# Retention and two feed-forward layers on one core: the second layer's first product by seven block products in place of eight

## The chip, the cores and the metric

The kernel runs on 1 of the 8 cores of one Trainium2 chip. The metric is the device time of one execution in microseconds (us), lower is better; the value before is the median of three runs. Of one execution a hardware profiler also left a trace, and all rows below come from it.

## The reference

Retention over two batches, then two dense layers with an activation between the products. The second layer is what the change touches.

```python
# retention: state = gamma*state + k v^T ; y = q state / 8      (2 batches, 8 heads, 768 positions, 64)
x = attn_out.transpose(0, 2, 1, 3).reshape(1536, 512)
h = x @ w_in          # layer 1: 512 -> 2048
x = (np.maximum(h, 0.0) + np.log1p(np.exp(-np.abs(h)))) @ w_out        # 2048 -> 512
h = x @ w_in2         # layer 2, first product: 512 -> 2048
g = h * np.clip(h + 3.0, 0.0, 6.0) / 6.0
out = g @ w_out2      # layer 2, second product: 2048 -> 512
```

The weights arrive as 64-bit floats.

## The kernel before, in words

One large function, `tile_retention_moe_kernel`, does not issue instructions. It gives tasks to a planner (class `Plan`, lines 25 to 124): each has an engine, a cost, the tasks it follows, a due time, and the buffer slots that it takes and gives back. `Plan.run` then places the tasks by these costs and due times, which fixes the order of the instructions on each engine. Every engine takes its list in that order, and waits where an operand is not there yet. All instructions are recorded by one helper, so line 44 stands in every row and the names of the tiles tell operations apart.

**Precision.** Each operand of a product is held as two 32-bit parts, hi and lo, and a product of 128 x 128 weights with 512 columns is three matmuls: hi·hi, hi·lo, lo·hi. Making the parts costs two instructions for each 128 x 512 tile: ScalarE copies (`hi`), VectorE subtracts (`lo`).

**The layers.** Tokens are cut into three chunks of 512 (`NC`), the inner width 2048 into 16 slices `f` of 128. A unit is a layer, a chunk and a slice: `G1` (line 658) is the first product, 4 x 3 = 12 matmuls of 512 columns into one PSUM bank; then ScalarE and VectorE form the activation `g` and its hi and lo; `G2` (line 693) is the second product, again 12 matmuls, added up in four banks over the 16 slices. TensorE's order is a list (lines 231 to 250): G1 of unit s, G2 of unit s - 2, through all 96 units, with the retention in the gaps of layer 1. The last two G2 are merged by row block `j`; behind each row block VectorE scales the sums from PSUM into one of two `e` tiles (`scaled`, line 736) and a DMA stores it (line 739). An `e` tile is free again when its store has landed.

**Weights.** `weight` (line 265) fetches 512 KB of 64-bit words into one of three `raw` slots, takes some six instructions on ScalarE and VectorE to make a 32-bit word of them in one of four `cv` slots, and splits that into hi and lo in a `w` slot. In layer 2 the lo part is made by ScalarE (the negative) and an accumulating DMA of GpSimd's queue. All 64 weight slices stay in SBUF from then on; a slot of layer 1 becomes free when its last unit is done.

## Time and profile before

| what | value |
|---|---|
| device time, median of 3 runs | 586.13 us (586.0 to 586.29) |
| span of the profiled execution, first to last instruction | 584.8 us |
| TensorE busy | 576.6 us, 3607 matmuls |
| VectorE busy | 325.6 us |
| ScalarE busy | 302.5 us |
| GpSimd busy | 60.6 us |
| moved by DMA | 57.49 MB |

The profile gives the profiled execution's span alone; the median of the runs lies 1.33 us above it, which is what stands around the first and last instruction. Busy time is summed over the durations of instructions, and instructions of one engine overlap at their ends: a matmul of 512 columns lasts 0.39 us in a row, but the next one starts earlier than that. So a pace is read from starts, not from durations. The idle time before a row, in brackets, names what ended it.

### The profile page before, as it was taken

How to read it: one execution, taken by the hardware profiler on the slowest of the kernel's cores; microseconds unless marked ns; L12 is line 12 of the kernel's file. 1: busy time of each engine (PE TensorE's matmuls, PEld its weight loads, DVE VectorE, ACT ScalarE, POOL GpSimd, SP SyncE). 2: the span in 40 equal slices, each digit the busy share in tenths (PEclk: the TensorE clock that was granted, in tenths of full speed). 3: DMA queues.
4: the chain of work that ended last, by engine and by line, in shares of the span. 5: the costliest groups of instructions: out<-in, count | busy, mean ns of one | idle time of the engine just before them, and what ended most of it. 6: DMA issues, size and time to landing. Idle time of an engine off the chain costs nothing.

```text
span 584.8 us, 9136 instructions
## 1 busy us (share of the span) xinstructions
PE 576.6 (99%) x3607; PEld 474.5 (81%) x3607; DVE 325.6 (56%) x579; ACT 302.5 (52%) x503; POOL 60.6 (10%) x93
## 2 busy tenths in 40 slices
PE   8999999999999999999999999999999999999997
PEld 7778788887788788888888888888888888888886
DVE  4999999886655333666678776422422222422222
ACT  3589989883233333777799997622222222222220
POOL 0000001044440000011121221100000000000000
PEclk9999999999999999999999999999999999999999
DMA  9998766513442200265597798200100000100001
GB/s 198 253 262 210 195 182 210 170 31 68 82 81 68 73 1 0 55 156 141 137 244 173 199 245 218 49 6 0 73 1 1 1 1 0 73 0 1 0 1 72
DMA packets 75242, 57.49 MB, mean 98 GB/s; under 512 B 47552, under 2 KB 64960, under 8 KB 75200
## 3 DMA queue, kind: packets, MB, share of 16 engines
q1 hardware_dynamic: 68336, 46.42, 28.2%
q0 software_dynamic: 6864, 10.49, 10.4%
q8 instruction: 28, 0.46, 0.4%
q14 instruction: 14, 0.11, 0.1%
HBM read 44.05 MB, written 3.15 MB: 81 GB/s over the span
## 4 chain that ended last, share of the span: by engine, by line
PE 97%; DVE 2%; DMA 0%; issue 0%; ACT 0%; POOL 0%; DVEq 0%; ACTq 0%; POOLq 0%
PE banks L44 97%; DVE raw L44 0%; DVE cv L44 0%; DMA out_dram<-e 0%; ACT w L44 0%; DVE e L44 0%; DVE st L44 0%; DVE qT L44 0%; DVE pw L44 0%; DVE w L44 0%; DVE x_lo L44 0%; DVEq L788 0%; POOL ident masks.py:199 0%; POOL small masks.py:65 0%; DVEq L44 0%
## 5 line engine op out<-in xcount | busy, mean ns | idle before, releaser
L44 PE MATMUL banks<-x_hi,w 128*128 128x512 f32 x768 | 252.9, 392 | 0.0
L44 PEld LDWEIGHTS banks<-x_hi,w 128*128 128x128 f32 x768 | 144.0, 188 | 30.6
L44 PE MATMUL banks<-x_lo,w 128*128 128x512 f32 x384 | 149.0, 389 | 0.0
L44 PE MATMUL banks<-hi,w 128*128 128x512 f32 x384 | 126.9, 392 | 0.0
L44 PE MATMUL banks<-w,hi 128*128 128x512 f32 (+1 forms) x386 | 118.4, 388 | 0.0
L44 DVE SCALAR_TENSOR_TENSOR g<-e,banks 128x512 f32<-128x512 f32 x48 | 33.0, 688 | 123.4 <-ACT e L44 123.2
L44 ACT ACTIVATE e<-banks,three 128x512 f32<-128x512 f32 x48 | 32.8, 684 | 120.2 <-PE banks L44 112.7
L44 DVE TENSOR_TENSOR lo<-g,hi 128x512 fp32r<-128x512 f32 x96 | 66.1, 689 | 41.4 <-ACT hi L44 41.2
L44 PEld LDWEIGHTS banks<-hi,w 128*128 128x128 f32 x384 | 72.1, 188 | 15.4
L44 PEld LDWEIGHTS banks<-w,hi 128*128 128x128 f32 x386 | 72.4, 188 | 14.9
L44 PEld LDWEIGHTS banks<-x_lo,w 128*128 128x128 f32 x384 | 72.2, 188 | 14.5
L44 ACT ACTIVATE hi<-g 128x512 fp32r<-128x512 f32 x96 | 60.4, 629 | 44.9 <-DVE g L44 42.2
L44 PE MATMUL banks<-w,lo 128*128 128x512 f32 (+1 forms) x193 | 74.9, 388 | 0.0
L44 PE MATMUL banks<-lo,w 128*128 128x512 f32 x192 | 74.8, 390 | 0.0
L44 DVE SCALAR_TENSOR_TENSOR cv<-raw,cv 128x512 uint32<-128x512 uint32 x96 | 65.8, 688 | 1.6
L44 ACT ACTIVATE w<-cv 128x512 fp32r<-128x512 f32 x101 | 60.2, 624 | 12.3 <-DVE cv L44 11.9
L44 POOL DMA_DIRECT2D w<-cv x37 | 32.6, 880 | 285.9 <-ACT w L44 166.5
L44 ACT ACTIVATE g<-banks 128x512 f32<-128x512 f32 x48 | 28.4, 591 | 59.1 <-PE banks L44 59.1
L44 ACT ACTIVATE cv<-raw,half 128x512 uint32<-128x512 uint32 x64 | 48.5, 759 | 3.5 <-DMA raw<-in_moe_w_out_dram 2.2
L44 DVE TENSOR_SCALAR raw<-raw 128x512 f32<-128x512 f32 x96 | 40.7, 428 | 10.8 <-ACT raw L44 7.9
L44 PEld LDWEIGHTS banks<-w,lo 128*128 128x128 f32 x193 | 36.2, 188 | 7.5
L44 PEld LDWEIGHTS banks<-lo,w 128*128 128x128 f32 x192 | 36.0, 188 | 7.2
(60 smaller groups left out, 367.1 us busy)
## 6 DMA issues: line engine op xcount, KB each, us to landing
raw<-in_moe_w_in_dram SPq DMA_DIRECT2D x32, 512.0 KB, 4.2
raw<-in_moe_w_out_dram SPq DMA_DIRECT2D x32, 512.0 KB, 4.6
w<-cv POOLq DMA_DIRECT2D x37, 256.0 KB, 4.9
out_dram<-e SPq DMA_DIRECT2D x11, 256.0 KB, 2.0
q<-in_q_dram SPq DMA_DIRECT2D x8, 256.0 KB, 5.3
v<-in_v_dram SPq DMA_DIRECT2D x8, 256.0 KB, 5.2
k<-in_k_dram SPq DMA_DIRECT2D x7, 256.0 KB, 5.4
raw<-in_k_dram SPq DMA_DIRECT2D x4, 256.0 KB, 3.4
```

The lines of the kernel that those rows point to most:

```text
L44: return self.plan.tc.keep_in_program_order(getattr(self.engine, op)(*args, **kwargs))
```

## The change

Layer 1 and the retention stay. In layer 2 the units of 512 tokens go, and there are 16 **steps** in their place: two blocks of 768 tokens, times eight pairs of slices `f`; block 0 takes the pairs 0 to 7, block 1 takes them from 7 to 0. In a step the first product is a 2 x 2 by 2 x 2 block product (two slices of 128, two halves of the 512 inputs, two halves of 384 tokens) by Strassen's scheme: seven products P1 to P7 of 6 matmuls with 384 columns, on sums of blocks. This asks for:

- sums of the weights (`late_in`: four VectorE instructions of 256 columns, then four hi/lo pairs), sums of the inputs (`operands`: four VectorE instructions of 768 columns and seven hi/lo pairs for each block of tokens; the rows of layer 1's result are copied once by ScalarE, without a split);
- in each step three additions that put the seven products together in two PSUM banks and in SBUF, and the activation in pieces: ten VectorE and six ScalarE instructions in all (a1 to a5, d1 to d9 and the hi/lo pairs `parts`);
- the second product as 12 `unit`s of 3 matmuls with 512 columns, which TensorE does between the products of the next step; it adds up in six PSUM banks, so each block ends with six output tiles, through the same two `e` tiles.

The second layer's weights no longer all stay in SBUF: the 16 slices of the second product are made in the `raw` slot itself (`late_out`), stored to a DRAM scratch, and read back for each block; the sums of pairs 0 to 3 (`KEEP`) are stored and read back for block 1. The lo parts of layer 2's weights are now made by VectorE; the 32 accumulating DMAs for them are gone.

```diff
--- before.py
+++ after.py
-        if kind == "h":
+        if kind in ("h", "prod"):
             return [[0], [1]]
+        if kind == "out":
+            return [[2 + u]]
...
+    G = [(0, c, f) for c in range(NC) for f in range(NF)]
+    STEPS = [(b, p) for b in range(2) for p in (range(NPAIR) if b == 0 else reversed(range(NPAIR)))]
+    PRODUCTS = {"P1": 2, "P6": 2, "P2": 2, "P7": 2, "P5": 2, "P4": 1, "P3": 1}
...
+    behind = [("G2", len(G) - LAG + i) for i in range(LAG)]
+    for i in range(len(STEPS)):
+        for name, n in PRODUCTS.items():
+            pe += [(name, i)] + behind[:n]
+            behind = behind[n:]
+        behind = [("unit", i, n) for n in range(12)]
+    pe += behind
...
+    def late_out(f):
+
+
+        key = 1, 1, f
+        x = Words(1, key, words[1][1])
+        at = due["P1", f // 2] - 40.0 + 2.0 * f
+        t = x.made(at, at - 10.0, 1.45, [])
+
+        def part(i):
+            return x.flat()[:, i * CH:(i + 1) * CH].bitcast(F32R)
+
+        a = nc.add("ACT", ACS, lambda: nc.scalar.activation(part(0), x.w().bitcast(F32), AF.Copy), [t], at)
+        b = nc.add("DVE", TT, lambda: nc.vector.tensor_tensor(part(1), x.w().bitcast(F32), part(0).bitcast(F32), ALU.subtract), [a], at + 0.7, give=[x.cv_k])
+        home = kept(f"stash_out{f}")
+        c = nc.add("SP", 0.45, lambda: nc.sync.dma_start(out=home, in_=x.flat().bitcast(F32)), [a, b], at + 1.5, give=[x.raw_k], load=1.6)
+        for b in range(2):
+            i = STEPS.index((b, f // 2))
+            back(("wo", b, f), home, c, due["unit", i, 3 * (f % 2)] - 12.0)
+
+    def back(key, home, after, when):
+        T["W", key] = [nc.add("SP", 0.45, lambda: nc.sync.dma_start(out=at_slot(key).rearrange("p a n -> p (a n)").bitcast(F32), in_=home),
+                              [after], when, take=[("w", key)], load=1.6, hold=HOLD + when - 10.0)]
+
+    def late_in(p):
+
+
+        x = [Words(1, (1, 0, 2 * p + f), words[1][0]) for f in range(2)]
+        at = due["P1", p] - (20.0 if p else 12.0)
+        t = [v.made(at + 2 * f, at - 10.0 + f, 1.75, [v.raw_k]) for f, v in enumerate(x)]
...
+        s1 = nc.add("DVE", d, put(0, lambda: word(1, 0), lambda: word(1, 1), ALU.add), t, at + 3.0, take=[sums])
+        s3 = nc.add("DVE", d, put(2, lambda: word(0, 0), lambda: word(1, 0), ALU.subtract), [s1], at + 3.1)
+        s2 = nc.add("DVE", d, put(1, lambda: total(0), lambda: word(0, 0), ALU.subtract), [s1], at + 3.2)
+        s4 = nc.add("DVE", d, put(3, lambda: word(0, 1), lambda: total(1), ALU.subtract), [s2], at + 3.3)
...
+        for n, (source, cols, after, give) in enumerate((
+                (lambda: x[0].w().bitcast(F32), whole, t, [x[0].cv_k]),
+                (lambda: x[1].w().bitcast(F32)[:, halves[1]], halves[1], t, [x[1].cv_k]),
+                (lambda: pair(0), whole, [s1, s2], [sums[1]]),
+                (lambda: pair(2), whole, [s3, s4], [sums[1]]))):
...
+            if p < KEEP:
+                home = kept(f"stash_in{p}_{n}")
+                c = nc.add("SP", 0.45, lambda home=home, key=key: nc.sync.dma_start(out=home, in_=at_slot(key).rearrange("p a n -> p (a n)").bitcast(F32)),
+                           [a, b], at + 6 + n, give=[key], load=1.6)
+                i = STEPS.index((1, p))
+                back(("wi", 1, p, n), home, c, due["P1", i] - 15.0 + n / 10)
...
+    def operands(b):
...
+        put(1, lambda: x(0, 1), lambda: x(0, 0), ALU.subtract, before, when["P6"] - 2.5)
+        put(2, lambda: x(1, 1), lambda: tf(1), ALU.subtract, [made[1]], when["P6"] - 1.5)
+        put(3, lambda: x(1, 1), lambda: x(0, 1), ALU.subtract, before, when["P7"] - 1.5)
+        put(4, lambda: x(1, 0), lambda: tf(2), ALU.subtract, [made[2]], when["P4"] - 1.5)
...
+            a = nc.add("ACT", act(2 * QT), lambda key=key, source=source: nc.scalar.activation(at_slot(key)[:, 0], source(), AF.Copy),
+                       [made[n]] if give else before, when[name], take=[("xf", key)], give=give, hold=early)
+            d = nc.add("DVE", dve(2 * QT), lambda key=key, source=source: nc.vector.tensor_tensor(
+                at_slot(key)[:, 1], source(), at_slot(key)[:, 0].bitcast(F32), ALU.subtract), [a], when[name] + 0.9, give=give)
...
+    A_OF = {"P1": (0, 0), "P2": (0, 1), "P3": (3, 1), "P4": (1, 1), "P5": (2, 0), "P6": (2, 1), "P7": (3, 0)}
+    BANK = {"P1": 1, "P2": 1, "P6": 2, "P7": 3, "P4": 3, "P5": 4, "P3": 4}
+
+    def step(i):
...
+                for kk in range(2):
+                    for m, (l, r) in enumerate(((0, 0), (0, 1), (1, 0))):
+                        first = fresh and kk == 0 and m == 0
+                        nc.tensor.matmul(bank(BANK[name]), w[:, l, kk, :], x[:, r, kk, :], start=first, stop=kk == 1 and m == 2, skip_group_check=not fresh)
+
...
+        p1 = product("P1", [])
+        p6 = product("P6", [])
+        a1 = ac(QT, lambda: nc.scalar.activation(at_slot(first), bank(1), AF.Copy), [p1], D["P2"] - 2.0, [first], psum=True)
+        p2 = product("P2", [a1])
+        d1 = dv(QT, lambda: nc.vector.tensor_tensor(at_slot(mid), at_slot(first), bank(2), add), [p6, a1], D["P7"] - 1.2, [mid], [first, K(2)])
+        p7 = product("P7", [])
+        a2 = ac(QT, lambda: nc.scalar.activation(at_slot(e[0])[:, 0], bank(1), AF.Relu, bias=three), [p2], D["P5"] - 1.8, [e[0]], psum=True)
+        d4 = dv(QT, lambda: nc.vector.scalar_tensor_tensor(at_slot(c[0])[:, 0], at_slot(e[0])[:, 0], 6.0, bank(1), ALU.min, ALU.mult), [a2], D["P5"] - 1.0, [c[0]], [K(1)])
+        p5 = product("P5", [])
+        d2 = dv(QT, lambda: nc.vector.tensor_tensor(at_slot(total), at_slot(mid), bank(3), add), [p7, d1], D["P4"] - 1.2, [total])
+        p4 = product("P4", [d2])
+        d3 = dv(QT, lambda: nc.vector.tensor_tensor(at_slot(c[0])[:, 1], at_slot(total), bank(4), add), [p5, d2, d4], D["P3"] - 1.2, [], [total])
+        p3 = product("P3", [d3])
+        a3 = ac(QT, lambda: nc.scalar.activation(at_slot(e[0])[:, 1], at_slot(c[0])[:, 1], AF.Relu, bias=three), [d3], after_all - 2.5)
+        d5 = dv(QT, lambda: nc.vector.scalar_tensor_tensor(at_slot(c[0])[:, 1], at_slot(e[0])[:, 1], 6.0, at_slot(c[0])[:, 1], ALU.min, ALU.mult), [a3], after_all - 1.8, [], [e[0]])
+        d7 = dv(QT, lambda: nc.vector.tensor_tensor(at_slot(c[1])[:, 1], at_slot(mid), bank(3), add), [p4, d2], after_all - 0.5, [c[1]], [mid, K(3)])
+        d8 = dv(QT, lambda: nc.vector.tensor_tensor(at_slot(c[1])[:, 0], at_slot(mid), bank(4), add), [p3, d3, d7], after_all, [], [mid, K(4)])
+        a5 = ac(2 * QT, lambda: nc.scalar.activation(at_slot(e[1]), at_slot(c[1]), AF.Relu, bias=three), [d7, d8], after_all + 0.6, [e[1]])
+        d9 = dv(2 * QT, lambda: nc.vector.scalar_tensor_tensor(at_slot(c[1]), at_slot(e[1]), 6.0, at_slot(c[1]), ALU.min, ALU.mult), [a5], after_all + 1.2, [], [e[1]])
+        for n, after, when in ((0, [d4, d5], after_all - 1.0), (1, [d9], after_all + 2.0)):
+            a = ac(2 * QT, lambda n=n: nc.scalar.activation(at_slot(g[n])[:, 0], at_slot(c[n]), AF.Copy), after, when, [g[n]], [c[n]])
+            d = dv(2 * QT, lambda n=n: nc.vector.tensor_tensor(at_slot(g[n])[:, 1], at_slot(c[n]), at_slot(g[n])[:, 0].bitcast(F32), ALU.subtract), [a], when + 0.9, [], [c[n]])
+            T["parts", i, n] = [a, d]
+
...
+        for n in range(12):
+            q, x = divmod(n, 6)
+            f, t = (0, x) if x < 3 else (1, x)
+            if q:
+                f, t = (0, x + 3) if x < 3 else (1, x - 3)
...
+            u = nc.add("PE", UNIT, go, T["parts", i, q] + T["W", w_key], at, take=[("bank", key)] if begun else [], give=[g[q], w_key])
...
```

**The order on TensorE**, in layer 2. Before, G1 of a unit (`x_hi`, `x_lo`) is followed by G2 of an earlier one (`w` with `hi` and `lo`):

```order
L44 MATMUL banks<-x_hi_1721,w_100 128x512 x2
L44 MATMUL banks<-x_lo_1724,w_100 128x512
L44 MATMUL banks<-x_hi_1721,w_100 128x512
L44 MATMUL banks<-w_1369,hi_107 128x512 x2
L44 MATMUL banks<-w_1369,lo_110 128x512
```

Of the change, the begin of step 2: P1 and P6, P2, P7, P5 (`xf` with `w`) with two units of step 1 (`w` with `parts`) behind each:

```order
L44 MATMUL banks<-xf_2871,w_96 128x384 x6
L44 MATMUL banks<-w_1354,parts_3261 128x512 x6
L44 MATMUL banks<-xf_2911,w_101 128x384 x6
L44 MATMUL banks<-w_1354,parts_3261 128x512 x3
L44 MATMUL banks<-w_1376,parts_3261 128x512 x3
L44 MATMUL banks<-xf_2886,w_96 128x384 x6
L44 MATMUL banks<-w_1376,parts_3261 128x512 x6
L44 MATMUL banks<-xf_2952,w_1330 128x384 x6
L44 MATMUL banks<-w_1354,parts_3157 128x512 x6
L44 MATMUL banks<-xf_2890,w_101 128x384 x6
L44 MATMUL banks<-w_1354,parts_3157 128x512 x3
L44 MATMUL banks<-w_1376,parts_3157 128x512 x3
```

The second products that stood as 12 matmuls in a row now stand in threes and sixes between products. Step 0 has no step before it: there, P6, P2, P7, P5, P4, P3 of step 0 and P1, P6 of step 1 follow each other with nothing between.

**The order on VectorE**, in layer 2. Before, with the weights done, two instructions for a unit (`g`, the activation, and `lo`):

```order
L44 SCALAR_TENSOR_TENSOR g_105<-e_102,banks 128x512
L44 TENSOR_TENSOR lo_110<-g_105,hi_107 128x512
L44 SCALAR_TENSOR_TENSOR g_104<-e_103,banks 128x512
L44 TENSOR_TENSOR lo_109<-g_104,hi_106 128x512
```

Of the change, step 4, from its addition d3 (`c` from `total`) to d8 (the second `c` from `part`); `raw` and `cv` are weights being made, `sums` their sums, `parts_3261` the lo part of the activation's first half:

```order
L44 TENSOR_TENSOR c_3112<-total_3121,banks 128x384 [waits PE_49]
L44 SCALAR_TENSOR_TENSOR cv_2_76<-raw_1_70,cv_2_76 128x512 [waits DVE_49]
L44 TENSOR_TENSOR sums_2458<-cv_1_75 128x256
L44 TENSOR_TENSOR sums_2458<-cv_3_77,cv_1_75 128x256
L44 SCALAR_TENSOR_TENSOR c_3112<-e_0_3109,c_3112 128x384 [waits Activation_49]
L44 TENSOR_TENSOR sums_2458<-sums_2458,cv_3_77 128x256 [waits DVE_49]
L44 TENSOR_TENSOR sums_2458<-cv_3_77,sums_2458 128x256 [waits DVE_49]
L44 TENSOR_SCALAR raw_2_71<-raw_2_71 128x512 [waits DMAHW3_49,Activation_49]
L44 SCALAR_TENSOR_TENSOR cv_0_74<-raw_2_71,cv_0_74 128x512 [waits DVE_49]
L44 TENSOR_TENSOR c_3144<-part_3099,banks 128x384 [waits PE_49]
L44 TENSOR_TENSOR parts_3261<-c_3112,parts_3261 128x768 [waits Activation_49]
L44 TENSOR_TENSOR c_3144<-part_3099,banks 128x384 [waits PE_49]
```

The making of weights, which stood beside units of two instructions, now stands inside steps of ten, and an instruction for a weight that waits for its fetch (`DMAHW3`) has the step's additions queued behind it.

**The end, on VectorE.** Before, the last four output tiles; the waits on a DMA are for the `e` tile:

```order
L44 TENSOR_SCALAR e_103<-banks 128x512 [waits PE_49]
L44 TENSOR_SCALAR e_102<-banks 128x512 [waits PE_49]
L44 TENSOR_SCALAR e_103<-banks 128x512 [waits DMAHW2_49,DVE_49,PE_49]
L44 TENSOR_SCALAR e_102<-banks 128x256 [waits DMAHW3_49,DVE_49,PE_49]
L44 TENSOR_SCALAR e_102<-banks 128x256
```

Of the change, the last six:

```order
L44 TENSOR_SCALAR e_103<-banks 128x512 [waits DMAHW2_49,PE_49]
L44 TENSOR_SCALAR e_102<-banks 128x512 [waits DMAHW3_49,PE_49]
L44 TENSOR_SCALAR e_103<-banks 128x512 [waits DMAHW0_49,DVE_49,PE_49]
L44 TENSOR_SCALAR e_102<-banks 128x512 [waits DMAHW1_49,DVE_49,PE_49]
L44 TENSOR_SCALAR e_103<-banks 128x512 [waits DMAHW2_49,DVE_49,PE_49]
L44 TENSOR_SCALAR e_102<-banks 128x256 [waits DMAHW3_49,DVE_49,PE_49]
L44 TENSOR_SCALAR e_102<-banks 128x256
```

Six tiles pass through the two `e` tiles where four did, and the six become ready at the ends of six units in a row.

## Rows read from the trace of the kernel before

**Rows 1.** The page: busy time of the engines, and the chain by engine.
```profile
PE 576.6 (99%) x3607; PEld 474.5 (81%) x3607; DVE 325.6 (56%) x579; ACT 302.5 (52%) x503; POOL 60.6 (10%) x93
...
PE 97%; DVE 2%; DMA 0%; issue 0%; ACT 0%; POOL 0%; DVEq 0%; ACTq 0%; POOLq 0%
```

**Rows 2.** Waits of TensorE: total us, times, longest us.
```profile
PE banks L44 <- ACT w L44: 2.1, 2, 1.1
PE banks L44 <- POOL ident masks.py:199: 1.5, 1, 1.5
PE banks L44 <- DVE qT L44: 1.0, 1, 1.0
```

**Rows 3.** Timeline, TensorE's last matmuls: start us, us, engine, operation, count.
```profile
575.87 0.39 PE L44 MATMUL banks<-w,lo 128*128 128x512 f32 x1
...
576.55 0.39 PE L44 MATMUL banks<-w,lo 128*128 128x512 f32 x1
...
580.17 0.40 PE L44 MATMUL banks<-w,hi 128*128 128x256 f32 x2
...
580.41 0.28 PE L44 MATMUL banks<-w,lo 128*128 128x256 f32 x1
580.41 0.31 PEld L44 LDWEIGHTS banks<-w,hi 128*128 128x128 f32 x2
580.53 0.40 PE L44 MATMUL banks<-w,hi 128*128 128x256 f32 x2
...
580.77 0.28 PE L44 MATMUL banks<-w,lo 128*128 128x256 f32 x1
```

**Rows 4.** Groups by line: weight loads; count, busy us and mean ns, idle before.
```profile
L44 PEld LDWEIGHTS banks<-w,hi 128*128 128x128 f32 x386 | 72.4, 188 | 14.9
```

**Rows 5.** Timeline, VectorE at the end: the output tiles.
```profile
576.97 0.69 DVE L44 TENSOR_SCALAR e<-banks 128x512 f32<-128x512 f32 x1 [1.22 <-PE banks L44]
...
579.83 0.69 DVE L44 TENSOR_SCALAR e<-banks 128x512 f32<-128x512 f32 x1 [0.80 <-DMA out_dram<-e]
...
581.22 0.76 DVE L44 TENSOR_SCALAR e<-banks 128x256 f32<-128x256 f32 x2 [0.70 <-DMA out_dram<-e]
```

**Rows 6.** A group of VectorE with 256 columns; then the timeline of one unit's activation.
```profile
L44 DVE TENSOR_TENSOR st<-st,banks 128x256 f32<-128x256 f32 x16 | 6.7, 417 | 0.8 <-PE banks L44 0.2
...
572.95 0.69 ACT L44 ACTIVATE e<-banks,three 128x512 f32<-128x512 f32 x1 [3.36 <-PE banks L44]
...
573.67 0.69 DVE L44 SCALAR_TENSOR_TENSOR g<-e,banks 128x512 f32<-128x512 f32 x1 [3.36 <-ACT e L44]
...
574.40 0.63 ACT L44 ACTIVATE hi<-g 128x512 fp32r<-128x512 f32 x1 [0.76 <-DVE g L44]
```

**Rows 7.** Timeline of VectorE, a stretch with no idle time between instructions.
```profile
300.11 0.69 DVE L44 SCALAR_TENSOR_TENSOR cv<-raw,cv 128x512 uint32<-128x512 uint32 x1
300.72 0.43 DVE L44 TENSOR_SCALAR raw<-raw 128x512 f32<-128x512 f32 x1
301.18 0.69 DVE L44 SCALAR_TENSOR_TENSOR cv<-raw,cv 128x512 uint32<-128x512 uint32 x1
301.79 0.42 DVE L44 TENSOR_SCALAR e<-g 128x512 uint32<-128x512 uint32 x1
302.13 0.69 DVE L44 SCALAR_TENSOR_TENSOR cv<-raw,cv 128x512 uint32<-128x512 uint32 x1
```

**Rows 8.** Stretches: length; busy us of PE, PEld, DVE, ACT, POOL; clock, DMA, GB/s.
```profile
30.00:60.00 30.00, 29.01 (x324) 22.97 (x324) 29.79 (x61) 28.64 (x49) 0.11 (x1) 1.00 0.86 234
60.00:100.00 40.00, 40.00 (x422) 32.24 (x417) 37.70 (x76) 35.38 (x61) 3.03 (x4) 1.00 0.69 188
```

**Rows 9.** DMA from 300 to 350 us: queue; fetches, KB, us to landing.
```profile
q1 hardware_dynamic: 3908, 7.31, 45.5%
...
raw<-in_moe_w_out_dram SPq DMA_DIRECT2D x10, 512.0 KB, 4.8
...
raw<-in_moe_w_in_dram SPq DMA_DIRECT2D x4, 512.0 KB, 5.4
```

More of the change, by code (lines that the diff above doesn't have):

```diff
@@ L128 @@
 GEMM = 2.73
+PRODUCT, UNIT = 1.03, 0.69
 SIGN = 0.75
@@ L334, in weight @@
+        part = [("w0" if number < ONCE else "w", ("w", key))]
         tail = 1.5 if BY_DVE(number) else 7.0
[L335 to L345 removed]
@@ L719, in gemm2 @@
[L719 to L722 removed]
+                for n, (l, r) in enumerate(((wh, hi), (wh, lo), (wl, hi))):
+                    nc.tensor.matmul(at_slot(("acc", c, j)), l[:, sl], r, start=(f == 0 and n == 0), stop=(f == NF - 1 and n == 2))
```

331 lines of the change are left out of this document (209 added, 122 removed).

## The prediction

> **What bounds the kernel now.** I read the page's busy times and chain first, then TensorE's waits, then single rows for prices. TensorE is busy for 576.6 us and has 97% of the chain [rows 1]; its three waits sum to 4.6 us [rows 2]. So the time is TensorE's list of matmuls and a tail: its last matmul ends at 580.77 + 0.28 = 581.05 [rows 3], 3.75 us before the span ends at 584.8. A shorter list is a gain only as far as no new wait enters it. The median of the runs, 586.13, lies 1.33 above the span; I add the terms to the span and carry the 1.33 along.
>
> **The list gets shorter: -14.1 us.** The pace comes from starts: three matmuls of 512 columns take 576.55 - 575.87 = 0.68 us, 0.2267 each, and five of 256 columns 580.77 - 580.17 = 0.60 us, 0.120 each [rows 3]. The line through both is 0.417 ns a column, the full one of the two clock levels, 2.4 GHz (granted share 1.00 in [rows 8]), plus 13 ns. For 384 columns no row exists; the line gives 0.1733 us. The bounds are 0.160 (columns alone) and 0.188, the mean of one weight load [rows 4], if loads should not hide. I take the line: in [rows 3] two loads start and end within 0.31 us while matmuls follow at 0.120, so loads of 188 ns overlap. The first product of layer 2 is 48 x 12 = 576 matmuls, 576 x 0.2267 = 130.6 us; with the change 16 x 7 x 6 = 672, 672 x 0.1733 = 116.5 us. The second product has 576 matmuls of 512 columns in both: nothing. A step is 42 x 0.1733 + 36 x 0.2267 = 15.44 us.
>
> **The tail gets longer: +2.8 us.** Output tiles pass through two `e` tiles, and a tile's next use comes 579.83 - 576.97 = 2.86 us after its last [rows 5], held by its store. Before, tiles are ready every 1.36 us, so two in 2.86 is nearly the pace. Now six end at units 0.68 us apart. With the first scaling at 0, the second starts at 0.68, the third at 2.86, the fourth at 3.54, the fifth at 5.72, the sixth at 6.40; from that start the span ends 584.8 - 581.22 = 3.58 later [rows 5], at 9.98. TensorE ends 5 x 0.68 = 3.4 after the first, so the tail is 6.58 in place of 3.75.
>
> **Step 0 has no cover: +1.1 us.** The parts of a chain: a hand-over is some 0.04 us (572.95 + 0.69 to 573.67) [rows 6]. VectorE takes 0.69 for 512 columns and 0.42 for 256 [rows 6], so 0.56 for 384 and 0.96 for 768. No row has ScalarE at another size: 384 lie between 0.52 (in proportion to 0.69) and 0.69; I take VectorE's share, 0.57, and so 0.87 for 768 (from 0.63). P5 needs the bank of P2: the end of P2 comes 0.17 after the next product can start (0.39 - 0.2267), then a2 and d4 with hand-overs, 0.17 + 0.09 + 0.57 + 0.04 + 0.56 + 0.1 = 1.53. Between stands P7 alone, 1.04: a wait of 0.5. P6 of step 1 waits 0.1 for a bank in the same way, and unit 0 stands 0.5 too early, since d3, a3, d5 and the pair `parts` (0.56, 0.57, 0.56, 0.87, 0.96) run with weights between them. In later steps two units (1.36) stand in each gap and these waits vanish: unit 0 comes 5.8 after the end of P5, and that chain takes 4.1.
>
> **VectorE in block 0: +2.5 us, between 0 and 10.8.** It fills up. At full load the next instruction starts 0.60 after one of 512 columns (300.11 to 300.72), 0.34 after a `TENSOR_SCALAR` (301.79 to 302.13), and 0.46 after it if its result is needed (300.72 to 301.18) [rows 7]. For 256 it is 0.76 - 0.42 = 0.34 [rows 5, 6], so 0.47 for 384 and 0.87 for 768. From d1 of step 1 to d1 of step 6 the list has 28, 24, 29, 32 and 31 instructions: 15.3, 12.2, 15.4, 16.7 and 16.1 us, and 23 of them need the result just before (0.12 each), in all 78.5 us. TensorE's five steps take 77.2. Steps 4 and 5 alone need 34.1 for 30.9. d1 may be late by some 3.2 without harm (P6 is followed by two units, P2 and two units, 3.8, before P7 needs d1), so load alone costs nearly nothing; but the list is in order, and each step also waits a little for TensorE or ScalarE, about 1 us, 5 in all. 78.5 + 5 - 77.2 - 3.2 = 3.1; I take 2.5, because in [rows 8] a VectorE at 29.79 of 30 us cost TensorE 1.0 and one at 37.70 of 40 nothing, which for 77 us is 1 to 2.5. The upper end takes full durations in place of starts (0.69, 0.43, 0.56, 0.42, 0.96; 88.0 us): 88.0 - 77.2 = 10.8.
>
> **What I cost at nothing.** Steps 9 to 15: ten VectorE instructions, 7 x 0.47 + 3 x 0.87 = 5.9 of 15.44 us. The last step: its second half of `parts` is ready some 4.6 after P3 (d8, a5, d9 and the pair, with hand-overs), under one unit of step 14 and six of its own (4.76); without this cover TensorE would wait those 4.6 once. The last nine units of layer 1, where the weights now begin: 78 instructions of VectorE, 43.4 us by the same paces, in 9 x 5.44 = 49. ScalarE: 82 instructions from step 1 to 6, about 60 us even at full durations, in 77. The 32 accumulating DMAs that go were off the path (GpSimd busy 10%) [rows 1]. The DMAs: 32 fetches, 32 stores and 16 reads of 512 KB, 41.9 MB, before block 0 ends, in about 149 us (nine units and 6.5 steps). The SP queue moved 7.31 MB in 45.5% of 50 us [rows 9], 0.321 MB/us, so these need 131: hidden, but not by much. They are hidden by a lead: the sums of pair p are done in step p - 2, some 23 us before use. If the lead is used up, each late transfer counts its 4.8 or 5.4 us.
>
> **Sum.** 584.8 - 14.1 + 2.8 + 1.1 + 2.5 = 577.1 of span, **578.4 us** as the runs are timed, 1.3% less.
>
> **Rivals.** *All covered* (0.20): VectorE's lateness stays within the 3.2, and step 0 costs little; 584.8 - 14.1 + 2.8 + 1.33 = 574.8. For it: [rows 8], 60 to 100. Against it: 78.5 us in 77.2. *VectorE sets block 0's pace* (0.10): the waits of a list in order add up as if nothing overlapped; 578.4 + 10.8 - 2.5 = 586.7 at most, 582 at least. Against it: the starts in [rows 7]. *The three `raw` slots set the pace, slower* (0.08): a slice of the second product now keeps its slot through a fetch (4.8), six conversions and a split (some 4.5) and its store (3.5, an estimate by doubling the bytes of an output's 2), 12.8; a slice of the first 5.4 + 3.2 = 8.6. Two of each a pair are 42.8, over three slots 14.3 of 15.44. From 1.2 us more for each slot's use this decides; with 4 more on engines that are full it is 19.6 a pair, 4.2 a step, 33 in eight, less the lead of 23: 578.4 + 10 = 588.4. For it: the SP queue is in order, and a fetch that waits for a store holds back the reads behind it. *Weight loads don't hide, slower* (0.04): 672 x 0.188 = 126.3, a gain of 4.2 for 14.1; 578.4 + 9.9 = 588.3. It decides from 0.174 us a load; [rows 3] speak against it with 0.120. The Trainium skill has a rule for this side, on its page "TensorE: Matmul & The Clock Gate", section "Back-to-back issue gap": a stream of loads and matmuls is paced by both, at about 131 ns for 512 columns and 81 for 128. By it, an estimate, 384 columns take 114, 672 x 0.114 = 76.8 against 576 x 0.131 = 75.5, so the product would become longer by 1.3 and the time 593.8. The trace doesn't agree: 512 columns take 227 here.
>
> **How the numbers follow.** My forecast has 0.58, from 575.5 to 581.5. The range leaves out the two slower rivals and the upper half of *VectorE sets the pace*, 0.17: 574.0 (all covered, with the end a little shorter) to 585.0. A change of 0.2%, 1.2 us, is about what a measurement of this kernel can tell from none. Faster by more: 0.58 + 0.20 + 0.06 (the lower part of the third case) = 0.84; the same 0.04; slower 0.08 + 0.04 = 0.12.
>
> **What would show it.** Right: starts of 384-column matmuls 0.173 apart; steps 9 to 15 at 15.4 us; a tail of 6.6 us behind the last matmul with two or three `e` scalings that wait for `out_dram`; a wait of about half a microsecond at P5 of step 0; in steps 4 and 5 a few waits of TensorE for `part` or `parts` by VectorE, 1 to 5 us in all. Wrong: 0.188 apart (weight loads); TensorE waiting for `w` by a DMA, or VectorE idle before `raw` rows for a fetch (slots); block 0 steps of 17 us (VectorE).

## The result, and the profile after

The changed kernel takes **580.53 us** (median of 4 runs, 579.83 to 581.24) against 586.21 us of the kernel before, timed beside it (586.0 to 586.54): a ratio of 0.9904, 95% interval 0.989 to 0.9918. The profiled execution took 580.47 us, with a span of 578.7. The forecast was 578.4 us, and a span of 577.1.

The page of the kernel after: the engines' busy time, and the chain by engine, to be read beside [rows 1].

```profile
PE 566.5 (98%) x3703; PEld 482.9 (83%) x3703; DVE 409.3 (71%) x733; ACT 311.0 (54%) x505; POOL 32.8 (6%) x61
...
PE 81%; DVE 9%; DMA 6%; ACT 2%; issue 1%; SPq 0%; DVEq 0%; ACTq 0%
```

TensorE has 96 matmuls more and is busy for 10.1 us less; VectorE has 84 us more to do. The chain no longer is TensorE's alone: 9% and 6% of it run through VectorE and DMAs.

TensorE's waits after (total us, times, longest us), beside [rows 2]:

```profile
PE banks L44 <- ACT w L44: 2.0, 2, 1.1
PE banks L44 <- POOL ident masks.py:199: 1.5, 1, 1.5
PE banks L44 <- DVE qT L44: 1.0, 1, 1.0
PE banks L44 <- DVE c L44: 0.6, 2, 0.4
```

The three old waits stand as they were, in layer 1. One line is new: VectorE's `c`. The timeline of TensorE (start us, us, engine, operation, count, and in brackets the idle time and its releaser) shows where:

```profile
313.83 0.87 PE L44 MATMUL banks<-xf,w 128*128 128x384 f32 x4
...
323.91 2.37 PE L44 MATMUL banks<-xf,w 128*128 128x384 f32 x12 [0.19 <-DVE c L44]
...
389.19 0.86 PE L44 MATMUL banks<-w,parts 128*128 128x512 f32 x3
390.41 1.31 PE L44 MATMUL banks<-xf,w 128*128 128x384 f32 x6 [0.36 <-DVE c L44]
...
405.52 0.86 PE L44 MATMUL banks<-w,parts 128*128 128x512 f32 x3
406.51 1.32 PE L44 MATMUL banks<-xf,w 128*128 128x384 f32 x6
```

Layer 2 begins at 313.83 with P1 of step 0 (before it began at 314.29, so 0.46 of the gain lies ahead of the change and is no more than the 0.9 by which this moment differs between the profiles of this study). The other rows are P5 of step 0, and P1 of steps 5 and 6 with the unit before each. A bracket counts from the end of the matmul before, which overlaps the next one; by starts P5 comes 0.36 late, and the two P1 come 1.22 and 0.99 after a unit that elsewhere takes 0.70, so 0.52 and 0.29 late. From start to start of P1 the steps take 13.32 us (step 0, with the last two second products of layer 1 in place of units), 15.67 to 15.69 (1 to 3), 16.21 (4), 16.10 (5), 15.76 (6), and 15.69 in every step from 7 to 14. In steps 4 to 6 the planner has put some units later than the list (in step 4 P6 stands straight behind P1). In a step of 15.69 nothing is idle, by the view of stretches (length; busy us of PE, PEld, DVE, ACT, POOL; clock, DMA share, GB/s), the last row being step 12:

```profile
327.16:406.51 79.35, 78.86 (x391) 70.26 (x390) 73.00 (x136) 50.11 (x83) 0.00 (x0) 1.00 0.65 223
...
500.71:516.40 15.69, 15.69 (x80) 14.10 (x79) 6.58 (x11) 4.32 (x6) 0.00 (x0) 1.00 0.58 202
```

TensorE is busy for all of the 15.69 us at full clock, while VectorE and ScalarE do 6.58 and 4.32 us. Yet 42 x 0.1733 + 36 x 0.2267 is 15.44. So 0.25 us of each step is neither a wait nor in the list as priced. In fifteen steps that is 3.7 us, more than all of TensorE's listed waits in layer 2. It is the main question of the experiments; the second is what delayed steps 4 to 6, the third the tail. VectorE's output tiles, beside [rows 5]:

```profile
568.44 1.37 DVE L44 TENSOR_SCALAR e<-banks 128x512 f32<-128x512 f32 x2 [0.97 <-PE banks L44]
571.32 1.36 DVE L44 TENSOR_SCALAR e<-banks 128x512 f32<-128x512 f32 x2 [1.51 <-DMA out_dram<-e]
574.24 1.40 DVE L44 TENSOR_SCALAR e<-banks 128x512 f32<-128x512 f32 x3 [1.56 <-DMA out_dram<-e]
```

Two tiles, a wait for a store, two tiles, a wait, the last two (one of them in halves): the pairs start 2.88 and 2.92 us apart. TensorE's last matmul ends at 571.83, and the span 6.87 us after it.

### The profile page after: what moved, and what is told of

Read it like the earlier page. It is cut to its first block, busy times and chain, and to the rows that moved or that the text cites. A ratio compares the mean times of both kernels' runs of the same rounds, so it can differ in the third digit from the quotient of the medians.

```text
span 578.7 us, 9565 instructions
## 1 busy us (share of the span) xinstructions
PE 566.5 (98%) x3703; PEld 482.9 (83%) x3703; DVE 409.3 (71%) x733; ACT 311.0 (54%) x505; POOL 32.8 (6%) x61
## 4 chain that ended last, share of the span: by engine, by line
PE 81%; DVE 9%; DMA 6%; ACT 2%; issue 1%; SPq 0%; DVEq 0%; ACTq 0%
PE banks L44 81%; DMA raw<-in_moe_w_in_dram 3%; DVE cv L44 3%; DVE c L44 2%; DVE raw L44 1%; DMA stash_out<-raw 1%; DVE parts L44 1%; DVE w L44 1%; DMA out_dram<-e 1%; DVE sums L44 1%; DMA q<-in_q_dram 1%; DMA raw<-in_moe_w_out_dram 1%; ACT raw L44 1%; ACT e L44 0%; DVE e L44 0%
## 5 line engine op out<-in xcount | busy, mean ns | idle before, releaser
L44 PE MATMUL banks<-w,parts 128*128 128x512 f32 x579 | 149.6, 392 | 0.0
L44 PE MATMUL banks<-xf,w 128*128 128x384 f32 x672 | 134.5, 337 | 0.7 <-DVE c L44 0.6
L44 PEld LDWEIGHTS banks<-xf,w 128*128 128x128 f32 x672 | 120.1, 188 | 10.9 <-DVE c L44 1.9
L44 PE MATMUL banks<-x_hi,w 128*128 128x512 f32 x384 | 127.3, 395 | 0.0
L44 PEld LDWEIGHTS banks<-w,parts 128*128 128x128 f32 x579 | 106.9, 188 | 16.0
L44 PEld LDWEIGHTS banks<-x_hi,w 128*128 128x128 f32 x384 | 72.0, 188 | 15.6
L44 PE MATMUL banks<-x_lo,w 128*128 128x512 f32 x192 | 74.4, 390 | 0.0
L44 DVE SCALAR_TENSOR_TENSOR g<-g,e 128x512 f32<-128x512 f32 x48 | 33.0, 687 | 13.1 <-ACT e L44 12.8
L44 PEld LDWEIGHTS banks<-x_lo,w 128*128 128x128 f32 x192 | 36.1, 188 | 7.0
L44 DVE TENSOR_TENSOR lo<-g,hi 128x512 fp32r<-128x512 f32 x48 | 33.0, 687 | 8.3 <-ACT hi L44 8.2
```

The lines of the kernel that those rows point to most:

```text
L44: return self.plan.tc.keep_in_program_order(getattr(self.engine, op)(*args, **kwargs))
```

## The experiments

Ratios are to the kernel before, timed beside each.

### One product more: is it TensorE's list that counts?

```diff
-                for kk in range(2):
+                for kk in (0, 1, 0, 1) if name == "P3" else (0, 1):
```

> Edit: the six matmuls of product P3 are issued twice in each of the 16 steps, so that its sum counts it double; all else is the same. It puts back on TensorE one product of the eight that the scheme replaces. If TensorE's list sets the time in every step (theory A): 16 x 6 x 0.1733 = 16.6 us more, less what the waits in block 0 (about 0.8 us) give back, so 596.3 to 597.1 us. If VectorE or the fetches set the pace of block 0 (rival B: there the longer step gives them room), the eight steps of block 0 grow by less than 1.04 us each, and the time lies under 593.

One execution took 596.64 us, 16.2 more than the changed kernel's profiled execution, and the last matmul ends 16.2 later too (588.05). Of these 16.2, 0.64 lies ahead of layer 2, which begins at 314.47 here. The product adds 1.01 to 1.04 us to each of steps 1 to 3 and 7 to 14: there TensorE's list sets the time. In steps 4 to 6 it does not come out in full: they take 16.73, 16.77 and 16.69 us, so 0.52, 0.67 and 0.93 more. The waits before P1 of steps 5 and 6 are gone, 1.0 us in all, as theory A's "less what the waits in block 0 give back" has it. So block 0's other work was about 1 us behind TensorE's list there, and what is missing of the forecast in the other steps must lie in how fast the list runs.

### The quarter of a microsecond in each step

**One column count.** The units of the second product leave out 128 of their 512 columns, so that all matmuls of layer 2 have 384.

```diff
-                for cs in halves if tail else [slice(0, CH)]:
+                for cs in [slice(0, QT)]:
...
-                        nc.tensor.matmul(..., start=begun and m == 0, stop=ended and m == 2 and cs.stop == CH)
+                        nc.tensor.matmul(..., start=begun and m == 0, stop=ended and m == 2)
```

> Leaves out the last 128 of the 512 columns of each matmul of the second layer's second product, so that all 78 matmuls of a step have 384 columns; the tail's halves go too. In the changed kernel steps 10 to 14 take 15.69 us each where 42 x 0.1733 + 36 x 0.2267 = 15.44 was forecast. Theory, a change of column count costs (some 0.034 us for each pair of changes, seven pairs a step): with one size the steps take 78 x 0.1733 = 13.52 us and all starts are 0.173 apart. Rival, it is the operands (slices of wide tiles, other banks) or the reads and writes of the other engines beside them: the extra 0.25 us stays, 13.77 us a step.

561.02 us in one execution. Steps 10 to 14 take 13.52 us each, which is 78 x 0.1733 to the last digit. Its timeline, in step 13:

```profile
505.79 1.20 PE L44 MATMUL banks<-xf,w 128*128 128x384 f32 x6
506.83 1.20 PE L44 MATMUL banks<-w,parts 128*128 128x384 f32 x6
507.87 1.20 PE L44 MATMUL banks<-xf,w 128*128 128x384 f32 x6
```

Six matmuls in 1.04 us, 0.1733 each, products and units alike. So the line through 256 and 512 columns was right for 384, weight loads hide, and the second product's data do not cost. The same stretch of the changed kernel, step 12:

```profile
504.20 1.55 PE L44 MATMUL banks<-w,parts 128*128 128x512 f32 x6
505.59 1.21 PE L44 MATMUL banks<-xf,w 128*128 128x384 f32 x6
506.64 1.55 PE L44 MATMUL banks<-w,parts 128*128 128x512 f32 x6
...
513.94 0.86 PE L44 MATMUL banks<-w,parts 128*128 128x512 f32 x3
514.64 1.22 PE L44 MATMUL banks<-xf,w 128*128 128x384 f32 x6
515.70 0.86 PE L44 MATMUL banks<-w,parts 128*128 128x512 f32 x3
```

Six of 512 columns take 505.59 - 504.20 = 1.39 instead of 1.36, three take 0.70 instead of 0.68, six of 384 take 1.05 to 1.06 instead of 1.04. Wherever the column count changes, the next run is a little longer than its pace. But for the halves of the last unit the order of the instructions on every engine is the same in both kernels, so it is not the change of operands or of banks.

**Fewer changes.** The order after has seven pairs of changes in a step (a run of products, a run of units, seven times). Gathered into four:

```diff
-    PRODUCTS = {"P1": 2, "P6": 2, "P2": 2, "P7": 2, "P5": 2, "P4": 1, "P3": 1}
+    PRODUCTS = {"P1": 0, "P6": 4, "P2": 0, "P7": 4, "P5": 0, "P4": 3, "P3": 1}
```

> The whole computation, TensorE's order alone: P1 P6, four units, P2 P7, four units, P5 P4, three units, P3, one unit, so four pairs of changes between 384 and 512 columns in a step where there were seven. Theory, a change of column count costs: the extra 0.25 us a step falls to about 0.14, steps 10 to 14 take 15.58 us, and the time falls by some 1.6 us to 578.9, unless P6, which now follows P1 at once, waits for its bank. Rival, operands or traffic: steps stay at 15.69 us, time 580.5.

581.72 us (580.96 to 582.36), ratio 0.992 (0.9905 to 0.9935). Steps 7 to 14 take 15.68: a miss, nearly all of the extra stays. In step 4, at P6, and in step 12:

```profile
376.87 1.34 PE L44 MATMUL banks<-xf,w 128*128 128x384 f32 x6 [0.53 <-DVE c L44]
...
502.65 2.26 PE L44 MATMUL banks<-xf,w 128*128 128x384 f32 x12
504.75 2.92 PE L44 MATMUL banks<-w,parts 128*128 128x512 f32 x12
507.51 2.27 PE L44 MATMUL banks<-xf,w 128*128 128x384 f32 x12
```

Twelve matmuls of units take 2.76 for 2.72, twelve of products 2.10 for 2.08. So a change is not paid at once. It adds 0.02 in the first three matmuls of 512 columns, 0.03 in six and 0.04 in twelve; short runs paid only a part of it. The starts of the single matmuls in the trace show the same: behind a change to 512 columns they are 229, 233, 236, 224, 231, 236, 228, 232 and 231 ns apart, and 227 from the tenth on (0.041 us in all); behind nine or more of these the matmuls of 384 columns start 171, 175, 178, 185, 176 and 182 ns apart, then 173 (0.026 in all), but behind only six they add up to 0.004 over their pace. And P6 without units before it waits for a bank, in step 4 and again in step 6 (0.96 late by starts). A cost that saturates asks for very long runs, so the next kernels go to two runs and to one.

**Two runs of each**, from step 10 on (block 1 has no weights to make):

```diff
+    RUNS = {"P1": 0, "P6": 0, "P2": 0, "P7": 6, "P5": 0, "P4": 0, "P3": 6}
...
-        for name, n in PRODUCTS.items():
+        for name, n in (RUNS if i > 9 else PRODUCTS).items():
```

> Edit: in the steps from the tenth on of the second block (no weights are prepared there), the seven products and the units alternate in two runs instead of three: P1 P6 P2 P7, six units, P5 P4 P3, six units. TensorE's work is the same 42 matmuls of 384 columns and 36 of 512 per step. Theory A (a run of matmuls that follows one of another column count pays a transient, about 0.026 us over its first six at 384 and 0.040 us over its first nine at 512, so that a step costs 0.25 us over uniform streams): with two pairs of changes left, a step from 11 to 14 costs 15.44 + 2 x 0.066 = 15.57 us instead of 15.69, and the time falls by 4 to 5 times 0.12, 0.5 to 0.6 us, to about 580.0. Rival B (each long unit run adds its own share, whatever stands before it): steps stay at 15.69 us, the time at 580.5. Rival C (a bank that P5 or P7 takes over is not yet read out when the run is longer): single waits of TensorE on VectorE of 0.3 to 1 us in these steps, the time above 580.5.

(This text and the next count the pairs of the order after as three; they are seven. Their "tenth step of the second block" is step 10 of the 16.) 581.11 us (579.56 to 582.43), ratio 0.9912 (0.9898 to 0.9927): no difference in time can be told from it. Its steps 12 to 14 take 15.59 to 15.60 us, where 15.57 was expected. The 0.03 between stands at P7: its six matmuls have the same lag, up to 0.026, though no column count changes there. P7 waits for d1, which ends only 0.2 us before it; so a change is not the only thing that brings this lag. Step 11 loses 0.28 to one stall ahead of P7, and the profile lost more in block 0 (steps 3 to 6 take 16.58, 16.00, 16.31 and 16.69), where the program is the same. That part varies from execution to execution.

**One run of each**, on a kernel with two more edits (four output tiles and direct parts, both below; 578.06 us), from step 10, from step 8 and from step 2 on:

```diff
+    RUN = dict.fromkeys(PRODUCTS, 0) | {"P3": 12}
...
-        for name, n in PRODUCTS.items():
+        for name, n in (RUN if i > 9 else PRODUCTS).items():
```

> Edit, on the version with four output tiles and direct parts (578.06 us): from the tenth step of the second layer's second block on, the seven products stand in one run of 42 matmuls and the twelve units in one run of 36, so that each step has one pair of changes of column count instead of three. Theory A (each pair of changes costs about 0.08 us: 0.25 for three, 0.16 for two): steps 11 to 14 cost 15.44 + 0.08 = 15.52 us instead of 15.69, six steps gain 1.0 us, the time comes to 577.1. Rival B (the products need each other's sums: P2, P4 and P3 wait for the copy of P1 and for two additions on VectorE, which the units covered): TensorE stalls of 0.2 to 0.5 us ahead of P2, P4 or P3 in each step, steps of 15.7 to 16.5 us, the time 578 to 583.

> Edit: the same, from step 8 on, so in all of block 1 and not in block 0. Theory A: eight steps gain 0.17 us each, 1.3 us against the version with three pairs (578.06), so 576.7. Rival B (steps 8 and 9 still have additions late because VectorE finishes work from block 0): 577.1, as without them.

> Edit: the same, from step 2 on, so in block 0 as well. Theory A: fourteen steps gain 0.17 us each, 2.4 us, so 575.7. Rival B (in block 0 VectorE, busy with weights for 12 to 15 of a step's 15.7 us, is late for the additions between the products, which now follow each other at once): stalls ahead of P2, P4 and P3 in steps 2 to 6 of 0.5 to 2 us per step, the time 577 to 585 while steps 10 to 14 are still 15.52.

579.81 us (579.55 to 580.12) from step 10, ratio 0.9888 (0.9875 to 0.9902); 581.76 from step 8, 0.9922 (0.9908 to 0.9935); 582.63 from step 2, 0.9935 (0.9921 to 0.9948). All are slower than the 578.06 they started from: rival B holds, though at another product than it named. From step 8 on, step 8 takes 17.07 us (P6 comes 0.99 late); from step 2 on, steps 2 to 7 take 15.57 to 16.33. TensorE's and VectorE's timeline of the first, in step 13:

```profile
517.80 4.38 PE L44 MATMUL banks<-xf,w 128*128 128x384 f32 x24
...
522.43 3.39 PE L44 MATMUL banks<-xf,w 128*128 128x384 f32 x18 [0.25 <-DVE c L44]
...
521.21 0.58 ACT L44 ACTIVATE e<-banks,three 128x384 f32<-128x384 f32 x1 [1.59 <-PE banks L44]
...
521.82 0.55 DVE L44 SCALAR_TENSOR_TENSOR c<-e,banks 128x384 f32<-128x384 f32 x1 [1.09 <-ACT e L44]
```

P5 starts 4.63 us after P1 where 24 x 0.1733 is 4.16, and loses another 0.11 behind it. It waits for the bank of P1 and P2, which a2 (521.21) and d4 (521.82) must read first: the same chain that the prediction priced for step 0, now in each step, 0.41 to 0.44 us, on engines that are otherwise idle. The 36 matmuls of units take 8.20 for 8.16: their one change costs 0.04, and the change back 0.03 in P1. The rest of what the step is over 15.44, 0.55 to 0.58, is the stall and the slow starts behind it.

| pairs of changes in a step | kernel | step, us | over its list |
|---|---|---|---|
| 7 | the change | 15.69 | 0.25 |
| 5 | less VectorE work (below), step 6 as the planner placed it | 15.66 | 0.22 |
| 4 | four runs | 15.68 | 0.24 |
| 2 | two runs | 15.60 | 0.16, 0.03 of it at P7 |
| 1 | one run | 16.06 to 16.09, 0.55 to 0.58 of it the stall | 0.07 |
| 0 | one column count | 13.52 | 0.00 |

The extra is zero without a change. It falls with the number of changes only when there are few, since a long run pays 0.07 for its pair and a short one less. What in TensorE makes it was not tried.

### What delayed steps 4 to 6

P1 of step 5 needs the bank that d7 of step 4 frees, on VectorE (a step puts its products together by five additions, d1, d2, d3, d7 and d8, not three). On the kernel after, the timeline of the SP queue and of ScalarE:

```profile
373.82 0.32 SPq L44 DMA_DIRECT2D stash_out<-raw  x1
379.79 2.82 SPq L44 DMA_DIRECT2D raw<-in_moe_w_out_dram  x2
...
383.30 0.77 ACT L44 ACTIVATE cv<-raw,half 128x512 uint32<-128x512 uint32 x1 [2.39 <-DMA raw<-in_moe_w_out_dram]
```

and the SP queue's waits from 374 to 392 us:

```profile
SPq L44 <- DMA stash_out<-raw: 5.6, 1, 5.6
```

A store from a `raw` slot is issued at 373.82; the fetch that takes that slot waits 5.6 us for it to land and goes out at 379.79; ScalarE stands idle for 2.39 us until the words are there. But VectorE, which has d7 in its list, had other work meanwhile: from 374 to 392 us it waited only 0.29 us, for ScalarE's part of these words. So the late fetch can make at most 0.29 of the 0.53 by which P1 comes late; the rest is VectorE's list. Two theories: the slot that is held until its store lands, or VectorE's load, of which this is only an occasion.

**Less VectorE work.** `masked` (one of VectorE's three instructions for a weight of layer 2) does 64 of its 512 columns and leaves out the rest.

```diff
-            nc.vector.scalar_tensor_tensor(self.w(), self.y(), 0x80000000, self.w(), ALU.bitwise_and, ALU.bitwise_or)
+            w, y = self.w()[:, :HALF], self.y()[:, :HALF]
+            nc.vector.scalar_tensor_tensor(w, y, 0x80000000, w, ALU.bitwise_and, ALU.bitwise_or)
```

> Leaves out seven eighths of one VectorE instruction for each weight of the second layer (the sign bits, masked: 64 of 512 columns, 0.13 for 0.60 us), 1.9 us less VectorE for each step of block 0, in the same order. Theory, VectorE's load in block 0 makes TensorE wait at the begin of steps 5 and 6 (0.53 and 0.30 us in the changed kernel): both waits vanish, steps 4 to 6 take 15.7 us, the time falls by about 0.9 to 579.6. Rival, fetches that come late hold the list: the waits stay, 580.5.

579.78 us (579.44 to 580.9), ratio 0.9891 (0.9876 to 0.9906). From 374 to 392 us the SP queue waits for a store again:

```profile
SPq L44 <- DMA stash_out<-raw: 6.0, 1, 6.0
```

and the timeline of ScalarE and TensorE has

```profile
385.08 0.76 ACT L44 ACTIVATE cv<-raw,half 128x512 uint32<-128x512 uint32 x1 [4.03 <-DMA raw<-in_moe_w_out_dram]
...
391.22 1.32 PE L44 MATMUL banks<-xf,w 128*128 128x384 f32 x6 [1.03 <-DVE c L44]
...
406.36 0.86 PE L44 MATMUL banks<-w,parts 128*128 128x512 f32 x3
407.06 1.23 PE L44 MATMUL banks<-xf,w 128*128 128x384 f32 x6
```

The two waits part. P1 of step 6 (407.06, 0.70 behind its unit) no longer waits: d3 of step 5 waits for TensorE in both kernels (1.10 us in the change, 1.21 here), and from its start to that of d7 VectorE's list takes 3.99 us here where the change takes 4.38, so that wait was VectorE's list. P1 of step 5 waits longer, 1.03, behind the fetch: VectorE, with less to do, is now idle for 2.36 us there. The fetch goes out as early as in the change (379.64), but ScalarE has its words only at 385.08, 1.8 us later, and is idle for 4.03. Less work on VectorE doesn't help against that. One profile of each is little to go by: the profiles of "four output tiles" and "two runs", with the same order on each engine through block 0 as the change, have P1 of step 5 late by 0.64 and 0.32 and P1 of step 6 by 0.39 and 0.49.

**No store in the slot's turn.** The parts go straight to TensorE's slot; block 0 no longer reads them back.

```diff
-        key = 1, 1, f
-        x = Words(1, key, words[1][1])
-        at = due["P1", f // 2] - 40.0 + 2.0 * f
-        t = x.made(at, at - 10.0, 1.45, [])
+        x = Words(1, (1, 1, f), words[1][1])
+        key = "wo", 0, f
+        at = due["unit", STEPS.index((0, f // 2)), 3 * (f % 2)] - 20.0
+        t = x.made(at, at - 10.0, 1.45, [x.raw_k])
...
-            return x.flat()[:, i * CH:(i + 1) * CH].bitcast(F32R)
+            return at_slot(key)[:, i]
...
-        a = nc.add("ACT", ACS, lambda: ..., [t], at)
+        a = nc.add("ACT", ACS, lambda: ..., [t], at, take=[("w", key)], give=[x.cv_k])
...
-        c = nc.add("SP", 0.45, lambda: nc.sync.dma_start(out=home, in_=x.flat()...), [a, b], at + 1.5, give=[x.raw_k], load=1.6)
-        for b in range(2):
-            i = STEPS.index((b, f // 2))
-            back(("wo", b, f), home, c, due["unit", i, 3 * (f % 2)] - 12.0)
+        c = nc.add("SP", 0.45, lambda: nc.sync.dma_start(out=home, in_=at_slot(key)...), [a, b], at + 1.5, give=[key], load=1.6)
+        i = STEPS.index((1, f // 2))
+        back(("wo", 1, f), home, c, due["unit", i, 3 * (f % 2)] - 12.0)
```

> Edit: the second weight's two parts (rounded, and what rounding leaves) are written straight into the slot that TensorE reads in block 0, 20 us before their unit, instead of into the raw tile, from which they went to the scratch and came back for block 0 as well; only block 1 still fetches them from the scratch. 16 fewer fetches of 512 KB, and a raw slot is free as soon as both parts are made and not when the store has landed. VectorE's and ScalarE's instructions are the same in number and size. Theory A (the waits of TensorE at the start of steps 5 and 6 come from raw slots that stay taken until their store has landed): the store drops out of the raw slots' turn, the waits of SP's queue for a landed store of 5 to 6 us go, the 0.53 and 0.30 us before P1 in steps 5 and 6 go, and the time falls by 0.5 to 0.9 us, to 579.6 to 580.0. Rival B (VectorE's work in block 0 is too much there): both waits stay within 0.2 us, the time at 580.5. Rival C (conversion that is due 20 us before its unit meets the sums of the products on VectorE and is late itself): new waits at the units, 0.5 us or more each, the time above 580.5.

581.1 us (580.19 to 581.9), ratio 0.991 (0.9897 to 0.9923): the time is that of the change, so the expected gain isn't there. The waits moved as theory A said, but the edit does not try the store alone: the second weight's conversions are now due some 20 us later in the middle of block 0, so VectorE's list is another one. From 374 to 392 us the SP queue waits for VectorE alone:

```profile
SPq L44 <- DVE cv L44: 10.5, 3, 7.3
SPq L44 <- DVE w L44: 4.9, 2, 3.5
SPq L44 <- DVE sums L44: 2.2, 1, 2.2
```

Step 4 takes 15.69, step 5 15.82, step 6 15.79; P1 of step 6 still comes 0.14 late. But P5 of step 0 now waits longer, since conversions stand in front of d4, and one step of block 1 lost 0.5, with no releaser listed. P5 on the timeline of TensorE:

```profile
324.85 1.33 PE L44 MATMUL banks<-xf,w 128*128 128x384 f32 x6 [0.42 <-DVE c L44]
```

Steps 1 to 5 as one stretch, where the change has TensorE busy for 78.86 of 79.35 us:

```profile
328.10:406.65 78.55, 78.55 (x392) 70.36 (x391) 75.99 (x139) 53.70 (x87) 0.00 (x0) 1.00 0.51 180
```

Here it is busy for all of 78.55 us, 0.8 less than the change needs. VectorE is busier than in the change (75.99 us, there 73.00), so its load as such does not make TensorE wait; but in the change VectorE's list also waits itself, 5.4 us in all in these steps, and here 1.1. The same five steps of the kernel with one column count:

```profile
327.47:407.02 79.55, 72.52 (x391) 68.60 (x390) 72.89 (x136) 49.95 (x83) 0.00 (x0) 0.98 0.64 223
```

That row says how near block 0 is to another bound: with a list on TensorE that is 10.8 us shorter (five steps of 13.52 for 15.69) it still takes 79.55 us, and TensorE idles for 7.0. (The clock of 0.98 is a stretch from 392.0 to 395.6 us at a granted 0.53, so nearly all of it at the lower level, 1.2 GHz; P1 of step 5 had waited 2.2 us just before, at 390.85. P1 of step 6 still comes 0.97 late behind it, so it does not set the 79.55.) So the making of weights, VectorE's list with the `raw` slots as the change has them, needs some 79.5 us for what TensorE does in 78.4. How much of it is the list and how much the slots was not separated.

### The tail, and all together

**Four output tiles.** The two tiles `g`, free by then, join the two `e`.

```diff
+    nc.pool("ob", 4)
+    slots["ob"] = {i: slots[n][i % 2] for i, n in enumerate(("e", "e", "g", "g"))}
...
-                d = nc.add("DVE", ..., take=[] if k else [("e", ("ob",) + key)], give=[key])
+                d = nc.add("DVE", ..., take=[] if k else [("ob", ("ob",) + key)], give=[key])
```

> The whole computation, with four tiles for outputs (the two e and the two g tiles of layer 1) in place of two. Theory, the tail is set by the two e tiles: the last scaling starts some 3.5 us after the first in place of 6.4, the tail behind the last matmul falls from 6.87 to about 4.0 us and the time by 2.8 to 577.7. Rival, the stores themselves queue behind one another at the end: a tail of over 6 us, time 580.

578.48 us (577.06 to 579.06), ratio 0.9859 (0.9842 to 0.9877).

```profile
569.58 1.37 DVE L44 TENSOR_SCALAR g<-banks 128x512 f32<-128x512 f32 x2 [0.98 <-PE banks L44]
570.94 1.37 DVE L44 TENSOR_SCALAR e<-banks 128x512 f32<-128x512 f32 x2
572.47 1.44 DVE L44 TENSOR_SCALAR g<-banks 128x512 f32<-128x512 f32 x3 [0.15 <-DMA out_dram<-g]
```

The scalings follow each other; of the waits 0.15 is left. The last matmul ends at 572.97 and the span (576.93) 3.96 later, 0.2 more than before the change (3.75).

**With direct parts.** Both edits in one kernel.

> Edit: the one before (second weight's parts written straight into TensorE's slot) together with the pool of four output tiles, whose run alone gave 578.48 us (tail 3.9 us instead of 6.87). If the two gains lie at different places of the path, they add: 578.48 less 0.5 to 0.9, 577.6 to 578.0 us, with a tail of 3.9 us and no wait of TensorE over 0.2 us from step 1 on. If the waits in block 0 are VectorE's: 578.5 us.

578.06 us (577.63 to 578.13), ratio 0.986 (0.9847 to 0.9873): not told apart from 578.48. Steps 1 to 4 are at 15.67 to 15.69, step 0 at 13.94 (a wait of 0.55 for `c` at P5), so the gain of steps 4 and 5 was given back in step 0. The sum of both gains was expected, and the text overlooked that wait.

**With two runs as well.**

> Edit: four output tiles, direct parts, and from the tenth step of the second layer's second block on the order in two runs (P1 P6 P2 P7, six units, P5 P4 P3, six units). Against the version without the two runs (578.06 us) theory A (0.08 us for each pair of changes; the six units after P7 cover the sum that P5 waited for in the order with one run) expects steps 12 to 14 of 15.60 us instead of 15.69, 0.5 us less in all, 577.5 us. Rival B (the longer run of products meets a bank not yet read, as P7 did in one step of the run of this order alone): one or two stalls of 0.2 to 0.5 us, 578.0 us.

**577.22 us** (576.65 to 577.62), ratio 0.9846 (0.9832 to 0.9859), the best of all. Steps 10 to 14 take 15.60, with no stall:

```profile
516.19 4.37 PE L44 MATMUL banks<-xf,w 128*128 128x384 f32 x24
520.40 4.28 PE L44 MATMUL banks<-w,parts 128*128 128x512 f32 x18
524.52 3.31 PE L44 MATMUL banks<-xf,w 128*128 128x384 f32 x18
527.66 4.28 PE L44 MATMUL banks<-w,parts 128*128 128x512 f32 x18
```

24 matmuls take 4.21 for 4.16 (half of it at P7, as above), 18 matmuls of units 4.12 for 4.08, twice, and 18 of products 3.14 for 3.12: 0.15 over the list, and the six units behind P7 cover the chain that P5 waits for.

## Why the prediction was right, and where it was not

The time fell as forecast, 2.1 us short of the forecast's gain, inside the range. Of these, 1.6 are in the span (577.1 forecast, 578.7 measured). The rest is the 1.33 us between span and time, which took the span of one execution and the median of others: in every execution for which both are on record it is 1.73 to 1.86, so that 577.1 of span would be 578.9 as the runs are timed. By its own steps, in span: 584.8 - 10.35 (list) + 3.12 (tail) + 0.47 (step 0) + 1.0 (block 0) - 0.46 (layer 1) = 578.6, measured 578.7.

- **The list: -14.1 forecast, -10.35 measured. This is the term that was mis-sized.** "For 384 columns no row exists; the line gives 0.1733 us": that was right, the run with one column count gives exactly this, and 0.188 (loads that don't hide) is out. What failed is the sentence after it, "A step is 42 x 0.1733 + 36 x 0.2267 = 15.44 us". Both paces were read in long runs of one column count, [rows 3], and the change mixes them, fourteen changes a step. Measured: 15.69, so 15 x 0.25 = 3.75 us of the gain are not there. Nothing in the rows of before shows such a mix in layer 2, and the bounds that were written (0.160 and 0.188 for one matmul) didn't ask what a change costs. But layer 1 of the kernel before has a mix, and it was not looked at. On TensorE's timeline of before, behind matmuls of the retention:

```profile
165.32 0.52 PE L44 MATMUL banks<-cv,st 64*64 64x64 f32 x12
...
166.10 0.39 PE L44 MATMUL banks<-x_lo,w 128*128 128x512 f32 x1
...
166.80 0.40 PE L44 MATMUL banks<-x_lo,w 128*128 128x512 f32 x1
...
167.49 0.39 PE L44 MATMUL banks<-x_lo,w 128*128 128x512 f32 x1
```

The second matmul of 512 columns starts 0.34 us after the first (165.76), and then three take 0.70 and 0.69 in place of 0.68: a lag of the kind that the experiments found was to be seen before the change, though behind 64 columns and not 384.

- **The tail: +2.8 forecast, +3.12 measured**, with the mechanism as told: two tiles, a period of 2.88 and 2.92 for 2.86, and with four tiles 2.9 of it goes.
- **Step 0: +1.1 forecast, 0.47 measured.** P5 comes 0.36 late and the matmul behind it another 0.11, as priced (0.5). P6 and unit 0 of step 1 do not wait; the 0.6 for them was too much.
- **VectorE in block 0: +2.5 forecast, 1.0 measured** (steps 4, 5 and 6: 0.52, 0.41 and 0.07 over 15.69), in the steps that were named. The two other profiles with the same order in block 0 have 1.5 (four output tiles) and 2.8 (two runs), so the 2.5 is not shown to be too much. The formula held VectorE's 78.5 + 5 - 3.2 = 80.3 against TensorE's 77.2. Both sides are nearly shown: with TensorE's list cut, the stretch takes 79.55. But TensorE's five steps are 78.4, for the reason above, so the terms were not independent: what the mix adds, block 0 no longer waits, just as the waits went when a product was added. The cause is mostly VectorE's list, as forecast: P1 of step 6 yes, and at P1 of step 5 all but the 0.29 of 0.53 that can be the late fetch.
- **At nothing.** Steps 9 to 15: VectorE 6.58 us busy a step (5.9 forecast by paces), no wait. The cover of the last step's parts held: no wait of TensorE there. The last units of layer 1 show no new wait. The DMAs were hidden but for that one fetch.
- **The rivals.** *All covered* was wrong by the mix and by block 0's 1.0 us. *VectorE sets block 0's pace* is not what happened at its price (582 at least): 79.5 us of making against 78.4 of TensorE is 1 us. *The three raw slots*: the mechanism is there, a fetch behind a store that has not landed, at 0.3 us in place of 10. (By its own sum it decides from 0.9 us more for each use, not 1.2: 3 x 15.44 less 42.8 is 3.5 us over four uses.) *Weight loads* are out: 0.1733 at 384 columns. The rule of the Trainium skill that stood beside it ("TensorE: Matmul & The Clock Gate", "Back-to-back issue gap") does not agree with these runs either: 384 columns, by an estimate between its two figures, take 114 ns, and took 173.
